# Moving the small steps of an attention front end within the slots of a two-layer matmul pipeline

## The chip, the cores and the metric

One core of one Trainium2 chip runs the whole program. The metric is the device time of a run in microseconds. "The span" is what the profile of one run covers, about 2.2 us less than the time of the same run.

## The reference

The computation is a recurrent attention cell (4 batches x 8 heads, 768 steps, head size 40) followed by a two-layer network with a squared ReLU (320 to 2048 to 320) on the 3072 resulting rows.

```
for t in range(S):
    m_new = maximum(f_gate[t] + m, i_gate[t])
    C = f_stab * C + i_stab * outer(v[t], k[t])
    n = f_stab * n + i_stab * k[t]
    y[t] = sigmoid(o_gate[t]) * (C @ q[t]) / maximum(abs(n . q[t]), 1)
x = y as (B*S, H*D)
out = (s * maximum(x @ w_in, 0)**2 + b) @ w_out
```

The gates as drawn make the state freeze after a few steps, so the kernel takes a short form of the cell (the first 42 keys suffice) and checks at run time, with a "flag", whether that was allowed.

## The kernel before

The 3072 rows are six **chunks** of 512, numbered 0 to 5. Chunks 0 to 3 hold middle rows of the four batches; chunks 4 and 5 hold the edge rows, of which those of the first 128 steps need real scores against the keys. A chunk has four **quads**, each with four **slots**: slots 0 to 15. During chunk c TensorE runs the first layer of chunk c and the second layer of chunk c - 1; between them, at given slots, come the small steps that make x for chunk c + 1. The order on every engine is the order of the program: no scheduler moves anything.

```python
for c in range(6):
    for k in range(4):                                       # a quad
        self.spare = f"o{(k + 1) % 2}" if c > 0 else "o1"     # the bank that this quad's sum does not use
        # ...
        self.mm1_rem(c, k, 0); self.mm1_rem(c, k, 1)          # 4 matmuls, first layer (rest of the depth)
        for a in range(2):
            self.mm1(c, k, a)                                 # 4 matmuls, first layer
            self.square(*prev)                                # VectorE: the square of the step before
            self.relu(c, k, a)                                # ScalarE
            prev = (c, k, a)
            for n, (f0, f1) in enumerate((((0, 3), (3, 6)), ((6, 11), (11, 16)))[a]):
                for e in at.pop((c, 4 * k + 2 * a + n), []):  # the small steps of this slot
                    e()
                self.mm2(c - 1, k, f0, f1)                    # second layer of the chunk before
```

`mm2` sums in bank `o0` or `o1` by the parity of the quad, and after its last matmul `osb` lets VectorE read the sum out. The small steps that matter:

```python
def ev_s(self, c, i):       # scores of an edge block: 3 matmuls, then masked out by VectorE
    ps = self.psO.tile([3 * L, 3, P], F32, tag=self.spare, name="ps_s")
    # ... 3 matmuls ps <- kbd, qt
    nc.vector.tensor_tensor(out=pm, in0=ps, in1=self.tri[...], op=ALU.mult)

def ev_h(self, c, i, early=False):  # 6 matmuls, then the normalising chain on VectorE
    # ... 6 matmuls ps_h <- pm,vall / qt,cn
    # d, dd, rec, fac, x, and a copy: six VectorE instructions

def make_tri(self):                 # 1 matmul in the spare bank, 1 VectorE copy
def flag_c(self): / flag_d(self):   # 1 small transpose each in the spare bank, read by VectorE
def tr_k(self):                     # DMA transpose of the keys, kt <- kp, in the SP queue
def ev_kt(self, bb):                # VectorE: kbd <- kt, for ev_s
def tr_q / tr_x:                    # DMA transposes of q and x, in the SP queue
def load_y(self, b0, eng):          # 8 loads of edge rows of q and o
```

## Time and profile before

| | before |
|---|---|
| median time, us | 145.24 (143.71 to 145.62, 4 runs) |
| span of the profile, us | 141.6 |
| TensorE busy | 93% |
| clean quad, us | 4.55 |
| quads with a hole, us | 6.14, 5.30, 6.29, 6.22, 5.31 |

The prediction shows where TensorE waits. What it waits for is seen in the timeline of VectorE around the longest wait of a score step. Columns: start, duration, engine, line, operation, output and inputs, shapes, and in brackets the idle time before it and what ended it.

```profile
73.43 0.17 DVE L341 SCALAR_TENSOR_TENSOR d<-ps_h,ib 128x16 f32<-128x16 f32 x1 [0.63 <-PE ps_h L333]
...
74.13 0.82 DVE L361 TENSOR_TENSOR fac<-ps_h,rec 128x640 f32<-128x640 f32 x1
75.04 0.83 DVE L365 SCALAR_TENSOR_TENSOR x<-th,fac 128x640 bf16<-128x640 f32 x1
75.91 0.20 DVE L370 COPY x<-x 128x128 bf16<-128x128 bf16 x1
76.01 0.54 DVE L485 SCALAR_TENSOR_TENSOR osb<-o,sc,brep 128x320 f32<-128x320 f32 x1
```

And TensorE at the same time, from its timeline:

```profile
73.93 0.61 PE L411 MATMUL hp<-xt,wr 64*128 64x512 bf16 x4
74.46 1.04 PE L423 MATMUL hp<-xt,wi 128*128 128x512 bf16 x4
76.61 0.33 PE L311 MATMUL ps_s<-qt,kbd 120*126 120x128 bf16 x3 [1.11 <-DVE osb L485]
```

The sum of the quad before was complete at about 73.9, when the next quad's matmuls began. Its read-out takes 0.54 us, but on VectorE it stands behind the six instructions of a normalising chain that began at 73.43, so the bank comes free only at 76.55. The score step asks for it at 75.4 and waits.

### The profile page before, as it was taken

What the parts mean: (1) busy time and instruction counts of PE and PEld (TensorE: products, weight loads), DVE (VectorE), ACT (ScalarE), POOL (GpSimd) and SP (SyncE); (2) the same over time, 40 slices, a digit from 0 to 9 for tenths busy, and PEclk for the clock granted to TensorE, in tenths of its full rate; (3) what the DMA queues carried; (4) which work ended last, traced back from release to release, by engine and by line L of the source; (5) the groups of instructions that cost most, each with busy time, mean ns of one, the idle gap of its engine ahead of it and who ended that gap; (6) DMA issues with size and microseconds to landing.
All of it is one profiled execution on the core that took longest, in us unless ns stands there. A gap on an engine that the chain in (4) does not pass through costs nothing.

```text
span 141.6 us, 2547 instructions
## 1 busy us (share of the span) xinstructions
PE 131.9 (93%) x960; PEld 75.0 (53%) x960; DVE 90.3 (64%) x200; ACT 69.6 (49%) x91; POOL 28.2 (20%) x58
## 2 busy tenths in 40 slices
PE   6999999999999999879996999997989999999980
PEld 6777634444564555354453555554545455547750
DVE  6779775969799647954379756578774453343320
ACT  3365678866556576633456454445343435532000
POOL 5997588000111107011011011100000000000000
PEclk9999999999999999999999999999999999999999
DMA  3999999922895899999996971103141100111121
GB/s 49 337 183 292 290 204 193 343 97 56 192 317 101 182 212 217 122 121 245 201 217 103 122 166 46 46 0 80 29 102 46 46 17 34 53 46 49 49 96 57
DMA packets 44236, 18.97 MB, mean 134 GB/s; under 512 B 33622, under 2 KB 43158, under 8 KB 44216
## 3 DMA queue, kind: packets, MB, share of 16 engines
q1 hardware_dynamic: 38268, 11.07, 41.4%
q0 software_dynamic: 5248, 7.55, 23.7%
q10 hardware_dynamic: 700, 0.11, 0.5%
q8 instruction: 9, 0.15, 0.4%
q14 instruction: 11, 0.09, 0.2%
HBM read 13.75 MB, written 3.93 MB: 125 GB/s over the span
## 4 chain that ended last, share of the span: by engine, by line
PE 70%; DVE 14%; DMA 7%; SPq 3%; issue 2%; ACT 1%; DVEq 0%
PE hp L423 24%; PE o L475 23%; PE hp L411 7%; PE o2t L475 6%; DMA kt<-kp 4%; DMA qx<-in_q_dram 3%; DVE x L365 3%; DVE fac L361 3%; PE ps_h L333 3%; DVE osb L485 2%; PE ps_w L545 2%; DVE g L437 2%; SPq L388 2%; PE ps_x L378 1%; PE ps_x L380 1%
## 5 line engine op out<-in xcount | busy, mean ns | idle before, releaser
L430 ACT ACTIVATE r<-hp 128x1024 bf16<-128x1024 f32 x48 | 48.9, 1023 | 51.0 <-PE hp L423 45.3
L475 PE MATMUL o<-wo,g 128*128 128x320 bf16 x320 | 51.5, 299 | 0.0
L423 PE MATMUL hp<-xt,wi 128*128 128x512 bf16 (+1 forms) x200 | 49.8, 372 | 0.0
L475 PEld LDWEIGHTS <-g 128*128 128x128 bf16 x384 | 36.6, 98 | 20.0 <-issue 1.9
L437 DVE TENSOR_TENSOR g<-r 128x1024 bf16<-128x1024 bf16 x48 | 32.4, 684 | 11.8 <-ACT r L430 11.6
L423 PEld LDWEIGHTS <-wi 128*128 128x128 bf16 x200 | 17.1, 98 | 22.8 <-issue 9.6
L485 DVE SCALAR_TENSOR_TENSOR osb<-o,sc,brep 128x320 f32<-128x320 f32 x20 | 11.0, 548 | 13.3 <-PE o L475 13.2
L497 POOL DMA_DIRECT2D out_dram<-osb x12 | 6.6, 553 | 57.5 <-DVE osb L485 43.6
L411 PE MATMUL hp<-xt,wr 64*128 64x512 bf16 (+1 forms) x100 | 15.7, 374 | 0.2 <-ACT xt L382 0.2
L365 DVE SCALAR_TENSOR_TENSOR x<-th,fac 128x640 bf16<-128x640 f32 (+1 forms) x14 | 10.2, 730 | 1.6 <-DVE fac L361 0.4
L361 DVE TENSOR_TENSOR fac<-ps_h,rec 128x640 f32<-128x640 f32 (+1 forms) x14 | 10.2, 728 | 0.4
L545 PE MATMUL ps_w<-ones 128*128 128x128 bf16 x100 | 8.8, 250 | 1.1 <-POOL ones L132 1.1
L475 PE MATMUL o2t<-wo,g 128*128 128x320 bf16 x64 | 8.9, 299 | 0.0
L545 PEld LDWEIGHTS <-ones 128*128 128x128 bf16 x100 | 7.5, 116 | 1.2 <-POOL ones L132 1.1
L411 PEld LDWEIGHTS <-wr 64*128 64x128 bf16 x100 | 3.5, 94 | 7.3 <-issue 6.6
L485 DVE SCALAR_TENSOR_TENSOR osb<-o2t,sc,brep 128x320 f32<-128x320 f32 x4 | 2.2, 551 | 5.7 <-PE o2t L475 5.7
L290 ACT ACTIVATE th<-ox 128x640 f32<-128x640 f32 x8 | 5.7, 730 | 0.0
L286 ACT CAST qb<-qx 128x160 bf16<-128x160 f32 (+1 forms) x11 | 4.2, 447 | 1.9 <-DMA qx<-in_q_dram 1.9
L333 PE MATMUL ps_h<-cn,qt 120*128 120x123 bf16 (+1 forms) x60 | 5.0, 212 | 0.1
L382 ACT COPY xt<-ps_x 128x384 bf16<-128x384 bf16 (+1 forms) x6 | 3.5, 584 | 2.9 <-PE ps_x L380 2.9
L333 PEld LDWEIGHTS <-qt 120*128 120x128 bf16 x60 | 3.7, 97 | 1.8 <-issue 1.0
L251 DVE TENSOR_TENSOR kbd<-kt,bdm 120x378 bf16<-120x378 bf16 x4 | 2.2, 546 | 2.2 <-DMA kt<-kp 2.2
(99 smaller groups left out, 80.5 us busy)
## 6 DMA issues: line engine op xcount, KB each, us to landing
out_dram<-osb POOLq DMA_DIRECT2D x12, 160.0 KB, 3.1
out_dram<-osb SPq DMA_DIRECT2D x12, 160.0 KB, 1.9
qx<-in_q_dram SPq DMA_DIRECT2D x2, 640.0 KB, 4.8
ox<-in_o_gate_dram SPq DMA_DIRECT2D x2, 640.0 KB, 6.2
qx<-in_q_dram POOLq DMA_DIRECT2D x2, 640.0 KB, 9.2
ox<-in_o_gate_dram POOLq DMA_DIRECT2D x2, 640.0 KB, 9.7
wo<-in_moe_w_out_dram POOLq DMA_DIRECT2D x4, 320.0 KB, 9.4
qy<-in_q_dram SPq DMA_DIRECT2D x8, 160.0 KB, 3.9
```

The lines of the kernel that those rows point to most:

```text
L290: self.nc.scalar.activation(out=th, in_=self.src("o", c, i), func=ACT.Tanh, scale=0.5)
L333: nc.tensor.matmul(ps[:, j, g * 123 : g * 123 + w], lhsT=lhs, rhs=rhs[:, g, :, :].rearrange("k a e -> k (a e)")[:, 0:w], start=True, stop= ...
L361: nc.vector.tensor_tensor(out=fac[:, j, :, :], in0=hv[:, j, :, 0:D], in1=rec[:, j, :].unsqueeze(3).to_broadcast([P, j.stop - j.start, H, D ...
L365: nc.vector.scalar_tensor_tensor(out=x[:, j, 0:DM], in0=th[:, j, :, :].rearrange("p j h d -> p j (h d)"), scalar=1.0, in1=fac[:, j, :, :]. ...
L411: nc.tensor.matmul(hp[:, e, n0:n1], lhsT=self.wr[64 * e : 64 * e + 64, k, a * P : (a + 1) * P], rhs=self.xt[64 * e : 64 * e + 64, t0:t1, 2 ...
L423: nc.tensor.matmul(hp[:, e, n0:n1], lhsT=self.wi[:, kt, f * P : (f + 1) * P], rhs=self.xt[:, t0:t1, kt, :], start=False, stop=(kt == 1),)
L430: self.nc.scalar.activation(out=r1, in_=self.hp.pop((c, k, a)), func=ACT.Relu)
L437: self.nc.vector.tensor_tensor(out=self.g[c][:, f : f + 3 : 2, :], in0=r1, in1=r1, op=ALU.mult)
L475: nc.tensor.matmul(self.o2[c, tb][:], lhsT=self.g[c][:, f, tb * P : (tb + 1) * P], rhs=self.wo[:, f, :], start=(f == 0), stop=(f == NF - 1),)
L485: nc.vector.scalar_tensor_tensor(out=osb, in0=self.o2.pop((c, tb)), scalar=self.sc[:, 0:1], in1=self.brep, op0=ALU.mult, op1=ALU.add)
L497: eng.dma_start(out=dst, in_=osb)
L545: self.nc.tensor.matmul(self.ps_w[:, 0:P], lhsT=self.ones[:], rhs=self.ones[:], start=True, stop=True)
```

## The change

Its intent: put the steps in the spare bank where that bank has been read out; bring the transpose of k forward, ahead of the edge loads; cast the edge q later. The core of the diff (the lines of unchanged context are cut):

```diff
@@ the places of cast, q transpose, tanh, chain (ev_h), x transpose, for blocks 0 and 1
                 2: (3, 4, 6, 7, 9, 3, 4, 8, 9, 11),
-                3: (-5, -4, 2, 4, 7, -4, -3, 4, 6, 9),
-            }.get(c, (-11, -10, 1, 3, 6, -10, -9, 4, 6, 9))
+                3: (-5, -4, 2, 4, 7, -4, -3, 4, 6, 10),
+            }.get(c, (-6, -5, 2, 4, 7, -5, -4, 6, 8, 11))
@@
-                put(d, 1, self.ev_s, c, 0)
-                put(d, 4, self.ev_s, c, 1)
+                put(d, 2, self.ev_s, c, 0)
+                put(d, 6, self.ev_s, c, 1)
@@
-        put(2, 8, self.make_tri)
-        put(2, 10, self.tr_k)
-        for c, b0 in ((3, 0), (4, 2)):
-            put(c - 1, 15, self.ev_kt, b0)
-            put(c, 2, self.ev_kt, b0 + 1)
+        put(2, 11, self.make_tri)
+        put(2, 1, self.tr_k)
+        for c, b0 in ((2, 0), (3, 2)):
+            put(c, 13, self.ev_kt, b0)
+            put(c, 15, self.ev_kt, b0 + 1)
@@
-        put(1, 15, self.load_rest2, self.nc.sync)
-        put(1, 15, self.load_y, 0, self.nc.sync)
-        put(2, 10, self.load_y, 2, self.nc.sync)
+        put(3, 12, self.load_rest2, self.nc.sync)
+        put(2, 1, self.load_y, 0, self.nc.sync)
+        put(2, 13, self.load_y, 2, self.nc.sync)
@@
-        put(4, 11, self.flag_c)
-        put(4, 13, self.flag_d)
-        put(5, 1, self.flag_e)
+        put(4, 13, self.flag_c)
+        put(4, 15, self.flag_d)
+        put(5, 2, self.flag_e)
```

So for chunks 4 and 5 the two chains move from slots 3 and 6 to 4 and 8, and the two score steps from 1 and 4 to 2 and 6. No instruction is added or removed.

## The prediction

> **What bounds the kernel now.** I read the busy shares first, then what TensorE (PE) waits for, then TensorE in order of time, then the stretches of that timeline side by side. From the page:
>
> ```profile
> PE 131.9 (93%) x960; PEld 75.0 (53%) x960; DVE 90.3 (64%) x200; ACT 69.6 (49%) x91; POOL 28.2 (20%) x58
> PEclk9999999999999999999999999999999999999999
> PE 70%; DVE 14%; DMA 7%; SPq 3%; issue 2%; ACT 1%; DVEq 0%
> ```
>
> TensorE carries the kernel, at full clock. But the chain of waits has 14% of VectorE (DVE) and 7% of DMA in it, so at some places TensorE is held. The list of waits of TensorE alone says where:
>
> ```profile
> PE ps_s L311 <- DVE osb L485: 2.1, 2, 1.1
> PE ps_tri L208 <- DVE osb L485: 1.4, 1, 1.4
> PE ps_w L545 <- POOL ones L132: 1.1, 1, 1.1
> PE ps_fl L523 <- DVE fl L516: 0.5, 1, 0.5
> PE hp L411 <- ACT xt L382: 0.2, 1, 0.2
> ```
>
> Columns: total us, times, longest. The kernel has six chunks (0 to 5) of four quads; a quad has four slots, so slots 0 to 15 per chunk. A quad is 4 remainder matmuls, 4 first-layer matmuls, 6 second-layer matmuls (slots 0, 1), 4 first-layer, 10 second-layer (slots 2, 3). The second-layer sum of quad k sits in bank o0 or o1 by k's parity; the other bank is "spare", and the small steps use it. It isn't really free early in a quad: VectorE's `osb` instruction still has to read the sum of the quad before out of it. That is the wait in lines 1 and 2.
>
> The list measures from a modelled matmul end, so I take the size of the loss from start to start: busy time by stretch, cut at the first remainder matmul of each quad (columns: stretch, length, then busy time of each engine, clock, DMA share, GB/s).
>
> ```profile
> 64.08:68.63 4.55, 4.55 (x30) 2.39 (x30) 1.84 (x3) 2.05 (x2) 0.57 (x1) 1.00 1.10 226
> 57.94:64.08 6.14, 4.75 (x30) 2.46 (x30) 4.11 (x9) 2.34 (x4) 0.60 (x1) 1.00 1.42 128
> 68.63:73.93 5.30, 5.19 (x40) 2.89 (x39) 3.58 (x9) 2.67 (x3) 0.54 (x1) 1.00 1.24 209
> 73.93:80.22 6.29, 5.18 (x38) 2.88 (x39) 5.28 (x12) 3.91 (x7) 0.54 (x1) 1.00 0.97 135
> 89.31:94.33 5.02, 5.02 (x38) 2.88 (x39) 3.29 (x8) 2.67 (x3) 0.54 (x1) 1.00 0.09 33
> 94.33:100.55 6.22, 5.18 (x38) 2.89 (x38) 5.21 (x12) 2.67 (x3) 0.00 (x0) 1.00 0.25 61
> 100.55:105.86 5.31, 4.81 (x30) 2.38 (x29) 4.14 (x13) 2.05 (x2) 0.00 (x0) 1.00 0.29 69
> 105.86:110.61 4.75, 4.75 (x31) 2.38 (x31) 1.99 (x4) 2.05 (x2) 0.00 (x0) 1.00 0.09 35
> ```
>
> The first row is a clean quad, 4.55 us. The others are chunk 2 quad 2, chunk 3 quads 0, 1, and chunk 4 quads 0 to 3. VectorE is never full in them (4.11 of 6.14, 5.28 of 6.29): it is late, not overloaded.
>
> **What the Trainium skill says.** "PSUM — Partial Sum Buffer", section "Engine vs sequencer instructions": the queues of VectorE and ScalarE are strict FIFO, and matmuls start and complete in program order. So a small matmul that waits holds all the second-layer matmuls behind it, and `osb` cannot pass the VectorE work queued before it. The trace agrees: ps_tri started at 60.90, right after `osb` ended (60.30 plus 0.54), and `osb` ran directly behind six instructions of the step before. "Perfetto Trace Analysis", section "Matmuls", says that independent groups should rotate through PSUM banks so that one is evacuated while the next computes. Here there are two such banks, and the small steps borrow one while it is being evacuated. "DMA: Bandwidth & Descriptors", section "Queues, rings and completion order": on each DMA engine descriptors are consumed in ring order. The trace agrees for the transpose of k: issued at 64.47, its user on VectorE starts only at 69.66, after other transposes of that queue.
>
> **The change part by part.** No instruction is added or removed; the orders of TensorE, VectorE, ScalarE and the DMA queue change. The matmul work stays the same, so the sum is holes closed minus holes opened.
>
> 1. *The tri step, slot 8 to 11* (chunk 2 quad 2). The quad is 6.14 and needs 4.55 plus 0.05 for its one 128-column matmul: **1.54** lost. In slot 11 TensorE arrives about 2.4 us later (0.81 for 6 matmuls, 0.86 for 4, 0.68 for 5), at about 61.8, and `osb` ended at 60.85. Hole closed.
> 2. *The two score steps (ps_s), slots 1, 4 to 2, 6, with the steps that use them at 4, 8 rather than 3, 6.* Chunk 3 and chunk 4 each contain 3 ps_s matmuls twice (0.17 each, from start to start) and 6 ps_h matmuls twice (0.32 each). Chunk 3 quad 0: 5.30 - 4.55 - 0.17 - 0.32 = **0.26**; quad 1: 6.29 - 5.04 = **1.25**. Chunk 4 quad 0: 5.02 - 5.04, nothing; quad 1: 6.22 - 5.04 = **1.18**.
> 3. *The flag steps, 11, 13 to 13, 15.* Chunk 4 quad 2: 5.31 - 4.55 - 0.10 for ps_fl = **0.66**, a wait for the VectorE work that makes fl. Quad 3: 4.75 - 4.55 = 0.20, all but 0.05 of it the ps_fm transpose itself.
> 4. *k's transpose, later loads and later casts.* None of these is on TensorE. VectorE idled 2.2 us for the transpose at 67.4 to 69.7, which delayed the `osb` ahead of the first score step: that is the 0.26 counted above. These moves buy the certainty that kbd is ready in slots 13, 15.
>
> Sum: 1.54 + 0.26 + 1.25 + 1.18 + 0.66 = 4.89, say **4.8 us**, less what opens anew.
>
> New order, worked out from row durations, time zero at the start of quad 1 in chunk 3 or 4. TensorE: the ps_h matmuls of slot 4 end at 1.83, ps_s of slot 6 at 3.67, the quad at 5.03. VectorE: the normalising chain d to copy takes 2.58 (73.43 to 76.01), so 1.93 to 4.51; a square 0.6 to 5.11; the masked copy of the scores (pm) to 5.66; `osb` to 6.2. TensorE needs pm, and the bank, in slot 8 at 5.03 + 1.51 = 6.54: 0.9 to spare. The second chain runs from 6.95 to 9.55. The DMA transpose of x then has until the next chunk at 5.03 + 4.87 + 4.55 = 14.45, so 4.9 us; in a quiet queue (81.72) it landed in 3.3. The tightest place is ps_fl in slot 13, in the first half of quad 3: in chunk 4, VectorE has chain (9.55), three reductions (0.79), a square (0.6), two small ones (0.33) and only then `osb` (0.55), so to 11.8; TensorE arrives at 9.90 + 1.51 + 0.41 = 11.82. I count **0.1** there. Casts: a relu with two casts behind it holds ScalarE 0.91 + 2 x 0.71 = 2.33, and the next relu comes 2.9 after it: no wait.
>
> **The rivals.**
> - *The wait moves.* Borrowed later, the bank must be given back sooner: pm has 2.9 us from ps_s to the next sum, with a 2.6 us chain queued before it. For it: VectorE is FIFO and busy 5.28 us in that quad. Against: the 0.9 above. If wrong, 0.5 to 1 us per chunk comes back, net gain about 3 us, 142.
> - *x arrives late at chunks 4, 5* because its last step moved from slot 6 to 8 and its transpose from 9 to 11. For it: transposes of x landed in 3.3 to 5.8 us; at 5.8 TensorE would wait 0.9. Against: the loads that crowd the queue (from 66 and from 49) are done or behind by then. At most 1.8 us: 142 again.
> - *The loads move into x's way in chunk 2*: the edge loads now start about 51 and take 6.8 us to issue, so chunk 3's first x transpose waits on them to about 58 and lands about 63 to 64, with chunk 3 at 67. Hidden, 3 us spare.
> - *Something else takes the time.* ScalarE is at 49%, VectorE at 64%: neither becomes the bound over 4.55 us.
>
> **Range and chances.** The median before is 145.19 (143.71 to 145.62), the span in the profile 141.6 in a run of 143.79. The span becomes 141.6 - 4.8 = 136.8; the median 145.2 - 4.8 = 140.4. Fast runs as before would give 139, a single rival 142. 2% is 2.9 us; half the gain would have to vanish to fall within it. Chances: faster 0.87, same 0.12, slower 0.01.
>
> **What would show it.** Right: no ps_s or ps_tri in TensorE's list of waits; chunk 2 quad 2 at 4.6, chunks 3 and 4 quads 0 and 1 at 4.7 and 5.0; VectorE's wait for kt gone; the part up to 48 us and after chunk 4 unchanged in length. Wrong: a wait of the second-layer sum o on pm (first rival), of hp on the DMA of x at a chunk's start (second), of ps_fl on `osb` of more than 0.3 us, or an early part that grew.

## The result, and the profile after

| | before | after |
|---|---|---|
| median time, us | 145.24 (143.71 to 145.62) | 139.79 (138.86 to 141.25) |
| ratio | | 0.962 (95%: 0.950 to 0.975) |
| span of the profile, us | 141.6 | 136.6 |

A ratio here is the mean time of one kernel's fast runs over that of the other's in the same rounds, so it is not quite the ratio of the medians. A run more than 1.5% above the fastest of its kernel is marked slow and left out of the ratios, though not of the medians: one of the four after the change (141.25) and one each of e5, e6, e7, e10 and e11 below. The change is faster by 3.8%. From the page of the profile after:

```profile
PE 130.8 (96%) x960; PEld 74.7 (55%) x960; DVE 90.5 (66%) x200; ACT 69.8 (51%) x91; POOL 28.3 (21%) x58
PE 92%; DMA 3%; DVE 1%; SPq 1%; ACT 0%; issue 0%
```

The chain that ends last is now 92% TensorE, where it was 70%; VectorE's share fell from 14% to 1%. The whole list of waits of TensorE after the change:

```profile
PE ps_w L545 <- POOL ones L132: 1.1, 1, 1.1
PE ps_q L299 <- DVE qb L286: 0.4, 1, 0.4
PE hp L411 <- ACT xt L382: 0.2, 1, 0.2
```

All three belong to the start of the program, before 16 us. ps_s, ps_tri and ps_fl are gone. The busy time by stretch, cut at the first remainder matmul of a quad as before: chunk 2 quad 2, chunk 3 quads 0 and 1, chunk 4 quads 0 to 3.

```profile
57.90:62.50 4.60, 4.60 (x30) 2.47 (x31) 4.12 (x9) 2.33 (x3) 0.60 (x1) 1.00 1.37 144
67.04:71.76 4.72, 4.72 (x32) 2.59 (x32) 2.40 (x4) 2.45 (x3) 0.54 (x1) 1.00 1.04 201
71.76:76.79 5.03, 5.03 (x39) 2.89 (x39) 3.95 (x9) 2.68 (x4) 0.54 (x1) 1.00 0.92 169
86.19:90.90 4.71, 4.71 (x32) 2.58 (x32) 2.40 (x4) 2.45 (x3) 0.54 (x1) 1.00 0.31 85
90.90:95.93 5.03, 5.03 (x39) 2.89 (x39) 4.03 (x9) 2.68 (x4) 0.00 (x0) 1.00 0.09 33
95.93:100.78 4.85, 4.85 (x35) 2.68 (x35) 4.39 (x13) 2.27 (x3) 0.00 (x0) 1.00 0.57 79
100.78:105.63 4.85, 4.85 (x31) 2.39 (x31) 3.36 (x11) 2.05 (x2) 0.00 (x0) 1.00 0.30 74
```

In each row the second number, TensorE busy, equals the length: no hole is left. VectorE has as much to do as before (4.12 against 4.11 in the first row), only in another order. Here is that order in quad 1 of chunk 3, from the timeline of VectorE:

```profile
71.87 0.55 DVE L485 SCALAR_TENSOR_TENSOR osb<-o,sc,brep 128x320 f32<-128x320 f32 x1 [0.80 <-PE o L475]
...
73.76 0.17 DVE L341 SCALAR_TENSOR_TENSOR d<-ps_h,ib 128x16 f32<-128x16 f32 x1 [0.74 <-PE ps_h L333]
...
76.95 0.55 DVE L316 TENSOR_TENSOR pm<-ps_s,tri 126x384 bf16<-126x384 f32 x1
77.41 0.54 DVE L485 SCALAR_TENSOR_TENSOR osb<-o,sc,brep 128x320 f32<-128x320 f32 x1
```

The read-out now runs first, at 71.87, as soon as the sum is complete, and the chain after it.

Run to run the times of one kernel spread over up to 2.8 us. Where that lies is seen when the span is cut in three: up to the start of chunk 2 (47.85 to 48.34 us in the four profiles of these two kernels), the middle from there to the last read-out of a sum, and the end. The middle is 89.70 us before and 84.75 after, a difference of **4.95 us**, and it repeats to 0.01 us between two of the three profiles of the changed kernel (the third is below); the kernel before has one profile. The middle ends where the last read-out starts. The end, from there to the last instruction, took 4.0 to 5.9 us for the same kernel. So the experiments are judged by their quads and their middle; the times are given with them.

### The profile page after: what moved, and what is told of

It reads as the page before. It is cut to its first block, busy times and chain, and to the rows that moved or that the text cites. A ratio compares the mean times of both kernels' runs of the same rounds, so it can differ in the third digit from the quotient of the medians.

```text
span 136.6 us, 2548 instructions
## 1 busy us (share of the span) xinstructions
PE 130.8 (96%) x960; PEld 74.7 (55%) x960; DVE 90.5 (66%) x200; ACT 69.8 (51%) x91; POOL 28.3 (21%) x58
## 4 chain that ended last, share of the span: by engine, by line
PE 92%; DMA 3%; DVE 1%; SPq 1%; ACT 0%; issue 0%
PE hp L423 33%; PE o L475 32%; PE hp L411 10%; PE o2t L475 6%; PE ps_h L333 3%; DMA qx<-in_q_dram 3%; PE ps_w L545 2%; PE ps_q L299 1%; PE ps_x L378 1%; PE ps_x L380 1%; PE ps_s L311 1%; PE ps_c L445 0%; DVE osb L485 0%; ACT xt L382 0%; DVE qb L286 0%; PE ps_b L463 0%
## 5 line engine op out<-in xcount | busy, mean ns | idle before, releaser
L475 PE MATMUL o<-wo,g 128*128 128x320 bf16 x320 | 50.8, 299 | 0.0
L346 DVE TENSOR_SCALAR d<-ps_h 128x16 f32<-128x16 f32 x8 | 1.4, 172 | 3.1 <-PE ps_h L333 3.1
```

Source lines behind the costliest of these rows:

```text
L475: nc.tensor.matmul(self.o2[c, tb][:], lhsT=self.g[c][:, f, tb * P : (tb + 1) * P], rhs=self.wo[:, f, :], start=(f == 0), stop=(f == NF - 1),)
```

## The experiments

All kernels gave the right result. Lengths of quads in us; "middle" as above; c2 q2 is chunk 2 quad 2.

| kernel | median time | ratio to before (95%) | c2 q2 | c2 q3 | c3 q0 | c3 q1 | c4 q0 | c4 q1 | c4 q2 | middle |
|---|---|---|---|---|---|---|---|---|---|---|
| before | 145.24 | | 6.14 | 4.55 | 5.30 | 6.29 | 5.02 | 6.22 | 5.31 | 89.70 |
| after | 139.79 | 0.962 (0.950 to 0.975) | 4.60 | 4.54 | 4.72 | 5.03 | 4.71 | 5.03 | 4.85 | 84.75 |
| e1 chain later | 141.04 | 0.974 (0.967 to 0.980) | 6.15 | 4.54 | 4.72 | 5.04 | 4.72 | 5.04 | 4.85 | 86.34 |
| e2 scores later | 141.79 | 0.978 (0.972 to 0.984) | 6.15 | 4.54 | 5.17 | 4.72 | 5.16 | 4.72 | 4.85 | 86.59 |
| e3 tri only | 143.80 | 0.992 (0.988 to 0.996) | 4.60 | 4.55 | 5.18 | 6.30 | 5.03 | 6.22 | 5.32 | 88.04 |
| e4 transfers only | 143.98 | 0.992 (0.988 to 0.996) | 6.15 | 4.54 | 5.03 | 6.29 | 5.02 | 6.22 | 5.32 | 89.43 |
| e5 all but transfers | 139.80 | 0.964 (0.953 to 0.975) | 4.60 | 5.33 | 4.72 | 5.03 | 4.71 | 5.03 | 4.85 | 85.56 |
| e6 flags early | 142.45 | 0.981 (0.968 to 0.994) | 4.60 | 4.55 | 4.71 | 5.03 | 4.71 | 5.03 | 7.08 | 86.87 |
| e7 x late | 143.44 | 0.988 (0.977 to 0.999) | 4.60 | 4.60 | 4.72 | 5.02 | 4.72 | 5.03 | 4.85 | 87.70 |
| e8 after again | 140.07 | 0.969 (0.958 to 0.980) | 4.60 | 4.90 | 4.72 | 5.02 | 4.72 | 5.02 | 4.86 | 85.11 |
| e9 split load | 140.23 | 0.963 (0.956 to 0.969) | 4.60 | 4.54 | 4.72 | 5.02 | 4.72 | 5.02 | 4.86 | 84.76 |
| e10 scores early | 140.60 | 0.960 (0.949 to 0.970) | 4.60 | 4.54 | 4.72 | 5.05 | 4.72 | 5.04 | 4.85 | 84.79 |
| e11 after, third | 140.60 | 0.959 (0.950 to 0.968) | 4.60 | 4.55 | 4.71 | 5.03 | 4.71 | 5.03 | 4.85 | 84.75 |

Two theories were tried. **Bank**: the spare bank isn't free in the first half of a quad, so the steps must go to the second half, as the change says. **Queue order**: the bank comes free about 0.7 us after a quad begins (72.42 against 71.76 in quad 1 of chunk 3 above) unless the read-out stands behind a long chain on VectorE; what counts is that the chain comes after the read-out.

### e1: the chains later, the score steps where they were

```diff
 # against the kernel before
-            }.get(c, (-11, -10, 1, 3, 6, -10, -9, 4, 6, 9))
+            }.get(c, (-11, -10, 2, 4, 7, -10, -9, 6, 8, 11))
-        put(4, 11, self.flag_c); put(4, 13, self.flag_d); put(5, 1, self.flag_e)
+        put(4, 13, self.flag_c); put(4, 15, self.flag_d); put(5, 2, self.flag_e)
```

> The kernel before with only the normalising chains of chunks 4 and 5 moved (from slots 3 and 6 to 4 and 8, with the flag steps that must follow them); the score steps stay in slots 1 and 4, in the first half of their quads. If the bank is simply not free in the first half of a quad, the score step of slot 4 still waits over 0.5 us in quad 1 of chunks 3 and 4, and the span stays above 140. If the wait is the queue order on VectorE (the read-out of the sum stands behind a 2.6 us chain), the chain now comes behind the read-out and both holes of about 1.2 us close with the score steps where they were: quad 1 of chunks 3 and 4 at 5.04 us, no wait of ps_s there, the flag hole of 0.66 closed, the tri hole of 1.5 and the 0.26 of chunk 3 quad 0 left; span 141.6 - 1.25 - 1.18 - 0.66 = 138.5.

The two stretches, quad 1 of chunks 3 and 4, from the busy time of e1:

```profile
73.43:78.47 5.04, 5.04 (x38) 2.87 (x38) 3.97 (x9) 3.37 (x6) 0.54 (x1) 1.00 0.50 104
92.59:97.63 5.04, 5.04 (x39) 2.87 (x39) 4.05 (x10) 2.67 (x4) 0.00 (x0) 1.00 0.10 36
```

TensorE is busy through both, with the score steps still in slots 1 and 4. The holes closed as queue order expected; the bank theory falls for the score steps. In slot 4 the chain's ps_h matmuls now come before the score step, which so asks 0.31 us later; that is not what closed the hole, for the bank was free at 74.09 and asked for at 75.15. The 0.26 of chunk 3 quad 0 went as well, which I had not expected: the transpose of k happened to land earlier in this run (kbd started at 67.86, against 69.66 in the kernel before).

### e2: the score steps later, the first chain where it was

```diff
 # against the kernel before
-            }.get(c, (-11, -10, 1, 3, 6, -10, -9, 4, 6, 9))
+            }.get(c, (-11, -10, 1, 3, 6, -10, -9, 6, 8, 11))
-                put(d, 1, self.ev_s, c, 0)
-                put(d, 4, self.ev_s, c, 1)
+                put(d, 2, self.ev_s, c, 0)
+                put(d, 6, self.ev_s, c, 1)
 # and the flag steps as in e1
```

> The kernel before with the score steps of chunks 3 and 4 moved to slots 2 and 6, the first chain left in slot 3 (the second one, which needs the second score step, in 8, and the flag steps behind it). The read-out of the sum still stands behind the first chain, but TensorE asks for the bank about 1.7 us later. Both views expect the holes of quad 1 to close; queue order says with about 0.7 us to spare. Span about 138.3 (141.6 - 0.26 - 1.25 - 1.18 - 0.66). If it stays above 140, then moving the step alone does not do it and the chain's place is what counts.

Quad 1 came down to 4.72 in both chunks, which is 4.55 and 0.17 of score matmuls: no hole. In chunk 3 the read-out still ran behind the first chain: the bank was free at 77.50 and asked for at 77.95, 0.45 to spare where 0.7 was expected. Quad 0, which holds the six ps_h matmuls, should be 5.04 and was 5.17 and 5.16. That leaves 0.12 to 0.13 in each. The list of waits doesn't name it, but the timelines place it: the masked scores (pm) were ready at 73.72 and 93.00, and the first ps_h matmul, which reads them, started at 73.77 and 93.06. The middle shrank by 3.11, where e1 gained 3.36. The span was 139.8 rather than 138.3; 1.1 us of that is a late start (chunk 2 began at 48.95), which has nothing to do with the edit. So asking later cures the hole too. Either move is enough by itself.

### e3: only the tri step

```diff
 # against the kernel before
-        put(2, 8, self.make_tri)
+        put(2, 11, self.make_tri)
```

> The kernel before with only the tri step moved from slot 8 to 11 of chunk 2. The simple sum of my prediction gives 141.6 - 1.54 = 140.1. If the transpose of k is what stands behind it, chunk 3 starts 1.5 us earlier but kbd still waits for a transpose that lands at 69.6, so the read-out ahead of the first score step ends at 70.7 while TensorE arrives at 69.0: a hole of about 1.7 us in chunk 3 quad 0 in place of 0.26, and the span stays at about 141.5.

The middle shrank by 1.66: 1.54 in chunk 2 quad 2, and 0.12 in chunk 3 quad 0. The simple sum was right and my fear of the transpose was not: kbd started at 68.16 here. With the transpose at its old place it started at 69.66 (before), 67.86 (e1), 69.67 (e2), 68.16 (e3) and 68.82 (e5), so its landing isn't a fixed time, and reading one profile's as a fixed time was the mistake. The span (141.5) hides the gain, because the end took 5.4 us in this profile against 4.0 before.

### e4: only the transfers, the casts and the kbd steps

```diff
 # against the kernel before
-            }.get(c, (-11, -10, 1, 3, 6, -10, -9, 4, 6, 9))
+            }.get(c, (-6, -5, 1, 3, 6, -5, -4, 4, 6, 9))
 # and tr_k, ev_kt, load_rest2, load_y as in the change
```

> The kernel before with only the transpose of k, the edge loads, the casts and the kbd steps moved as in the change; all steps in the spare bank stay. Both views: VectorE no longer waits for kt and the 0.26 of chunk 3 quad 0 goes, nothing else on TensorE moves: span 141.3, same within 2%. If the transfers were the main cause of the lateness of VectorE, the quad 1 of chunk 3 would shrink as well (by over 0.5).

The middle shrank by 0.27, all of it in chunk 3 quad 0 (5.30 to 5.03). No other quad changed by more than 0.02: the transfers were not what made VectorE late in quad 1. (The span was 141.8, not 141.3: it started 0.2 later, and the end was 0.3 longer.)

### e5: the change without its transfers

```diff
 # against the changed kernel
-            }.get(c, (-6, -5, 2, 4, 7, -5, -4, 6, 8, 11))
+            }.get(c, (-11, -10, 2, 4, 7, -10, -9, 6, 8, 11))
 # and tr_k, ev_kt, load_rest2, load_y as in the kernel before
```

> The changed kernel with the transpose of k, the edge loads, the casts and the kbd steps put back where they were before. If these moves only buy a margin, as the prediction says, the span stays at 136.6. If the transpose at its old place lands at 69.7, kbd and the read-out end at 70.7 and the first score step, for which TensorE arrives at 70.15, waits about 0.55 us: span 137.2.

A hole did open, of 0.78 us (chunk 2 quad 3 is 5.33 long, to the first matmul of chunk 3), but at another place than I named. From the list of waits of TensorE:

```profile
PE hp L411 <- DMA xt<-x: 0.7, 1, 0.7
```

It isn't the score step that waits for k, but the first matmul of chunk 3 that waits for the transpose of x. In the old order of the DMA queue the transposes of x stand behind the edge loads and the transposes of q. The second one was issued at 63.2 here as in the kernel before, but chunk 3 asks for it 1.5 us earlier, because the tri hole is gone, and that uses up what x had to spare. The transfers are worth 0.27 us alone and 0.8 us once the other holes are closed (0.45 against e8, the worse profile of the changed kernel). Which of the moved transfers does it was not tried.

### e6: the flag steps back

```diff
 # against the changed kernel
-        put(4, 13, self.flag_c); put(4, 15, self.flag_d); put(5, 2, self.flag_e)
+        put(4, 11, self.flag_c); put(4, 13, self.flag_d); put(5, 1, self.flag_e)
```

> The changed kernel with the flag steps back in slots 11, 13. A plain sum of parts says that this brings back the 0.66 us of before: span 137.3. Queue order on VectorE says more: the second chain now sits in slot 8, so the inputs of the flag are ready at 102.1 while TensorE arrives in slot 11 at 100.0, a hole of about 2.1 us in chunk 4 quad 2, span 138.7.

From its list of waits of TensorE:

```profile
PE ps_fl L523 <- DVE fl L516: 2.0, 1, 2.0
```

The hole is 2.0 us and not the 0.66 of before, as queue order said: moving the second chain from slot 6 to 8 pushes the flag's inputs behind it on VectorE. The move of the flag steps gains 0.66 of the 4.95, but without it the move of the chains would have cost 2.1 of it (the middle is 86.87 against 84.75). The span, 140.1, missed the expected 138.7: the end took 5.3 us in this profile.

### e7: x for chunk 4 four slots later

This one is made slower on purpose, to measure how much room the transpose of x has. It moves block 1 of chunk 4 only, whose chain runs during chunk 3.

```diff
 # against the changed kernel
                 3: (-5, -4, 2, 4, 7, -4, -3, 4, 6, 10),
+                4: (-6, -5, 2, 4, 7, -5, -4, 10, 12, 13),
```

> The changed kernel with the second chain of chunk 4 four slots later (12 instead of 8, its transpose in 13), about 4.55 us of TensorE's time. The prediction gave x 4.9 us to the start of the next chunk and 3.3 to 3.7 for its transpose to land, a slack of 1.2 to 1.6. Then a hole of 2.9 to 3.4 us opens at the start of chunk 4 and the span is 139.5 to 140. If the transposes needed the 5.8 us of the slowest one, there was no slack and the hole is over 4.5.

```profile
PE hp L411 <- DMA xt<-x: 2.8, 1, 2.8
```

Chunk 3 quad 3 grew to 7.72 (it holds 4.55 and the six ps_h matmuls, 0.32), so the hole is 2.85 us, just under the expected 2.9 to 3.4. What x has to spare follows from how much later its last transpose was issued. Counted from the start of chunk 3 that was at 19.19 us (86.41) here and at 14.37 (81.41) in the changed kernel: 4.82 later, more than the four slots' 4.54, because it now stood behind two loads in its queue. So the changed kernel has 4.82 - 2.85, about 2.0 us, to spare there, if the transpose lands there as it did here, 2.8 us after its issue; 1.2 to 1.6 was expected, from 3.3 to 3.7. The span of 141.3 was above the expected 139.5 to 140; the end took 5.6 us in this profile.

### e8 and e11: the changed kernel again

> The changed kernel itself, unedited, on the same chip as the three others, as the yardstick: span 136.6 within 0.1 in a run at full clock, time ratio to before 0.955 to 0.975.

> The changed kernel unedited, a third profile, as the yardstick on this chip for the two others. Span 136.6 to 137.3; the hole at the start of chunk 3 between 0 and 0.4 us; from the start of chunk 2 to the last read-out 84.7 to 85.1.

Both spans missed what was expected: 137.2 in e8 (0.36 in the middle, the rest a late start) and 139.0 in e11 (the end took 5.9 us). The middle was 84.75 in two of the three profiles of the changed kernel and 85.11 in e8, where the first matmul of chunk 3 waited for a DMA:

```profile
PE hp L411 <- DMA xt<-x: 0.3, 1, 0.3
```

In the first profile of the changed kernel the queue of the DMA issues (engine SP) in chunk 2 reads:

```profile
51.10 3.32 SPq L109 DMA_DIRECT2D qy<-in_q_dram  x4
54.52 5.66 SPq L109 DMA_DIRECT2D oy<-in_o_gate_dram  x4
60.28 3.84 SPq L396 DMA_TRANSPOSE xt<-x  x2
```

The second transpose of x was issued at 62.9 and took 3.7 us to land, so it was there at 66.6; chunk 3 began at 67.04. In e8 it was issued at 63.5 and took 4.1, and chunk 3 could have begun at 67.4. There is 0.4 us to spare or nothing.

### e9: the first edge load split around these transposes

```diff
 # against the changed kernel; load_y takes the names to load
-        put(2, 1, self.load_y, 0, self.nc.sync)
+        put(2, 1, self.load_y, 0, self.nc.sync, "q")
+        put(2, 10, self.load_y, 0, self.nc.sync, "o")
```

> The changed kernel with the first edge load split: its q half where the change put it, its o half behind the two transposes of x for chunk 3. In the two profiles of the changed kernel the second of these transposes was issued at 62.9 and 63.5, behind the o half, and chunk 3 started with a hole of 0.0 and 0.35 us. If the loads ahead of it are the cause, it is now issued by 61, lands by 65, about 2 us before chunk 3 asks for it, and no wait of TensorE for a DMA is left; the score transposes behind the o half are issued about 1 us later and still land before 70. From the start of chunk 2 to the last read-out of the sum: 84.7 us, as in the better of the two profiles of the changed kernel, against 85.1 in the other. The time itself: within 0.5 us of the changed kernel, not to be told from it. If something else delays x, the hole stays.

```profile
57.41 4.40 SPq L396 DMA_TRANSPOSE xt<-x  x2
61.90 3.15 SPq L109 DMA_DIRECT2D oy<-in_o_gate_dram  x4
```

Both transposes now go ahead of the o half (the second was issued at 60.6), and no wait for a DMA is left; the middle is 84.76, as in the better profiles of the changed kernel. The gain is at most the 0.35 us of e8, in those runs that have that hole. The time cannot show it: 140.23 against 140.60 for the changed kernel on the same chip, ratios 0.963 and 0.959, intervals overlapping. It is a safer order, not a measurably faster one, and no version beat the changed kernel.

### e10: the changed kernel with the score steps back in the first half

```diff
 # against the changed kernel
-                put(d, 2, self.ev_s, c, 0)
-                put(d, 6, self.ev_s, c, 1)
+                put(d, 1, self.ev_s, c, 0)
+                put(d, 4, self.ev_s, c, 1)
```

> The changed kernel with the score steps of chunks 3 and 4 put back into slots 1 and 4, in the first half of their quads, all else as changed. If the place of the chain behind the read-out is what counts, no wait of ps_s comes back and the span from the start of chunk 2 to the last read-out is 84.7 to 85.1, as in the changed kernel. If the second half of the quad is needed, as the change says, waits of over 0.5 us come back in quad 1 of chunks 3 and 4, 85.8 or more.

No wait of ps_s came back, the quads are the same to 0.02 us and the middle is 84.79. For the score steps the second half of the quad is not needed once the chains come after the read-out. This was not tried for the tri step: in e3 it was moved and its hole closed, but whether a later chain in chunk 2 would have closed it as well is open.

## Why the prediction was right, and where it wasn't

- **The time.** Predicted 140.4, with 139 and 142 named as likely ends; measured 139.79. The step that carries it, 4.8 us off the matmul timeline, measured 4.95 in the middle of the span. The medians differ by 5.45 us; the other 0.5 lies within the interval and is not explained. Two small slips: the median before is 145.24, not 145.19, which is one run; and to fall within 2%, 1.9 of the 4.8 us would have to vanish, less than half.
- **The parts.** Tri 1.54 predicted, 1.54 measured (also alone, e3). Chunk 3: 0.26 + 1.25 predicted; its four quads fell from 20.68 to 19.15, by 1.53. Chunk 4: 1.18 + 0.66 predicted; its quads fell from 21.30 to 19.44, by 1.86. Measuring from start to start was the right choice: the list of waits had 4.0 us for four of these holes, which are 4.63 from start to start, because it counts from a modelled end of the matmul before; the fifth, of 0.26, is not in it.
- **The wait does not move** (first rival). pm ended at 77.50, and TensorE reached slot 8 at 78.20: 0.7 to spare, 0.9 predicted.
- **x for chunks 4 and 5** (second rival). The chain ended at 81.39 and chunk 4 began at 86.19, so x had 4.8 us, 4.9 predicted; from the predicted 4.9 and 3.3 the slack is 1.6, and e7 put it at about 2.0, because the transpose landed in 2.8.
- **The flag.** I counted 0.1; there was none, but it is tight. From the timelines of VectorE and of TensorE after the change:

```profile
102.00 0.53 DVE L485 SCALAR_TENSOR_TENSOR osb<-o,sc,brep 128x320 f32<-128x320 f32 x1
```

```profile
102.60 0.27 PE L523 MATMUL ps_fl<-idf,fl 128*4 128x128 f32 x1
```

The bank was free at 102.53 and TensorE asked at 102.60, with no idle time noted. e6 shows what a slot earlier than the inputs allow costs.

- **Wrong: "Hidden, 3 us spare" for the first x transpose behind the edge loads** (third rival). The step that failed is "take 6.8 us to issue": that length was read off the kernel before, where these loads ran from 49.5 to 56.4. After the change they took from 51.10 to 60.18, 9.1 us, and both transposes of x stood behind them; I had not followed the second one at all. The spare time was 0.4 us in one profile and less than nothing, 0.35 us of hole, in another. The hole was small enough not to show in the time. Why the issue took longer isn't shown; only that it lay 1.6 us later beside other transfers.
- **Wrong in part: "It isn't really free early in a quad".** The prediction also said that `osb` stood behind six queued instructions, and that is the whole cause for the score steps of quad 1: in e1 and e10 they use the bank in the first half of the quad without a wait. I put the two statements side by side as if both were needed.
- **Too weak: "These moves buy the certainty that kbd is ready".** e4 puts 0.27 us on the transfers alone, as I had counted, but e5 shows 0.8 us in company, and for x rather than kbd.

## What to carry to other kernels

A step that waits for a buffer may be waiting for a queue, as here: look at what stands in front of the instruction that frees the buffer, and move that behind it, or ask later; either closed the hole of the score steps here. Size such holes from start to start against a clean period of the same loop, since waits counted from modelled ends understate them (4.0 for 4.63 us here). When several holes close at once, every later stage is asked for earlier, so re-check what each transfer has to spare with the new start times, and issue what the next stage needs ahead of bulk loads.

## What the Trainium skill lacked or had wrong

- "DMA: Bandwidth & Descriptors", section "DMA Transpose (X-bar)": it has constraints, but no time from issue to landing beside other traffic. Here the same 128 x 768 transpose of x within SBUF took 1.2 us to issue in a quiet queue and 2.4 to 2.7 behind loads, and landed 3.3 to 5.8 us after its issue in the profile of the kernel before and 2.8 after it in e7.
- "Perfetto Trace Analysis", section "DMA Instruction — HWDGE (DVE, Sync)": it says that a DMA's profiled time runs from the wait for the descriptor generator through the generation of the descriptors, without the movement of the data. It gives no size for how far this stretches beside other transfers: the same four loads of o took 3.74 us to issue in the kernel before and 5.66 after the change, with x behind them.
- "Perfetto Trace Analysis", section "Identifying Dependency Chains": it advises to look at the semaphore that an instruction waits on. Here that names the read-out (0.54 us), whose lateness came from the 2.6 us chain in front of it in VectorE's queue; "PSUM — Partial Sum Buffer", section "Engine vs sequencer instructions", has the FIFO rule; neither section joins the two.
- No page that I read gives the spread of a program's end: from the start of the last read-out of a sum to the last instruction took 4.0 to 5.9 us in three profiles of the same kernel.
